# A banded-attention and sine-MLP kernel on one core: batch 0's last x copies moved to ScalarE, its first matmuls started in the attention tail, GpSimd squares in the first MLP pass, and one step width in the last pass

## The chip, the cores and the metric

The kernel runs on one core of one Trainium2 chip. Its time is device microseconds (us) of one execution; of a kernel that was run several times, the median is given. An execution that was profiled has a span (first to last instruction of the trace) and, beside it, the same time as the others. TensorE is called PE in profiles, VectorE DVE, ScalarE ACT, GpSimd POOL, SyncE SP. PEld is PE's loading of weights.

## The reference

Attention in chunks of 32 queries with a little context and 8 memory keys, over 4 batches, 8 heads, 768 positions, 64 values a head; then, over the 3072 tokens with 512 features, an MLP whose activation is h + sin(alpha h)^2 / alpha:

```python
for c in range(nc):                       # 24 chunks of 32 queries
    k_ctx = k[:, :, l_start:r_end]        # 16 positions to the left, 8 to the right
    k_full = np.concatenate([mem_k, k_ctx], axis=2)
    v_full = np.concatenate([mem_v, v_ctx], axis=2)
    scores = scale * np.matmul(q_c, k_full.transpose(0, 1, 3, 2))
    a = softmax(scores)                   # written out with max, exp, sum
    out[:, :, c_start:c_end] = np.matmul(a, v_full)
x = out.transpose(0, 2, 1, 3).reshape(3072, 512)
h = x @ w_in                              # 512 x 2048
s = np.sin(alpha * h)
g = h + s * s / (alpha + 1e-09)
return g @ w_out                          # 2048 x 512
```

## The kernel before

**Stages.** The order on every engine is the order in which the program text issues instructions; nothing is rescheduled, and each engine works through its own queue in that order. There are four batches. For batch 0 the program first transposes k and q, then runs `burst(0)`, the attention; for each batch `i` there follows the first MLP layer ("pass i": 16 steps `ft`, each 128 of the 2048 hidden features, over the batch's 768 tokens), and beside it the second layer of the batch before and the preparation of the next. During pass 0 there is no second layer to interleave yet. After pass 0 come eight transposes (`t_k`, `t_q`, "pieces") for batch 1, mixed with second-layer matmuls of batch 0, and then `burst(1)`.

**Attention.** `burst` handles 8 blocks `j` of 96 queries in a software pipeline: scores and exp of block s (`qk_exp`, L262), the product with v of block s-lag (`pv`, L282: PE, then DVE's reciprocal L292 and scaling L293), and in the step after that `xt` (L300): four PE transposes (L306) and one DVE copy (L309) into `xT`, 96 of its 768 token columns. In batch 0, lag is 2, and one idle matmul (`spin`, L167) runs in each step.

**A step of the first layer** is `l1` (L333). PE makes hT with 8 matmuls (4 slices of 128 features, two halves of 384 tokens, L341). ACT makes u = sin(alpha h) (L353). The square s2 = u*u is made by the engine that a letter names: A for ACT (L356), D for DVE (L362), P for POOL (L358). Then DVE makes gT = s2/alpha + h (L370). The letters stand in one string for each pass:

```python
sq = ("ADADADAAADADADAA" if i == 0 else "ADAAPDADADAPADAD")[ft]
```

DVE's part (`finish`) of step ft is issued just before the matmuls of step ft+1. In PSUM, hT has a pool `big` of three buffers that scores, attention outputs and transposes share; in pass 0 the steps 3, 7 and 11 (`split`) use two buffers `hs` of the pool `smp` (two buffers) instead, and their Sin and gT run in two halves (L350, L366). u and s2 have three buffers each. So PE can't begin a step before DVE's gT of the third unsplit step before it is done.

**Second layer.** `l2` (L376) makes 128 tokens with 16 matmuls (L398) and hands each matmul back as one item of a `Stream`; the last item of a block also issues the copy out of PSUM (DVE L405 or ACT L407) and the store from SP's queue. `stream.take(n)` issues n items, and stops early at the end of a block, carrying the rest over. In passes 1 and 2 each step but the first is preceded by `take(2)`, in pass 3 by `take(3)`.

**Loads.** Weights, k, q and v are loaded and cast by DMAs issued from POOL's queue; the program's semaphores for them rotate over eight, so a load issued there waits until the one eight before it has landed. In order after the v blocks of batch 0: eight loads of w_in (256 columns each, L212), k and q of batch 1 (L115), four loads of w_out (4 steps' rows each, L218), four of v (L139 to L148). The memory values `memv_f` are cast once on ACT (L418, all batches, among the first transposes), and `put_memv` (L152, L153, DVE) spreads them into a v buffer for each batch.

**Tables.** ACT holds one table of functions at a time. The load for Sin stands just ahead of the first Sin of each pass, the load for Exp ahead of the first Exp of each burst; copies run under either.

Of the kernel before, what the change touches and what calls it, by code (L numbers as in the profile page):

```python
# [9 lines left out]
P = 128  # L10
QW = 96
# [3 lines left out]
F32 = mybir.dt.float32  # L15
# [30 lines left out]
def kernel(  # L46
# [12 lines left out]
    nc = tc.nc  # L59
    B, H, S, D = q.shape  # L60
# [6 lines left out]
    KT = d_model // P  # L67
    NSUB = S // P
    HALF = S // 2
# [7 lines left out]
    big = ctx.enter_context(tc.tile_pool(name="big", bufs=3, space=bass.MemoryType.PSUM))  # L77
    smp = ctx.enter_context(tc.tile_pool(name="smp", bufs=2, space=bass.MemoryType.PSUM))
# [13 lines left out]
    memv_st = consts.tile([P, B, H, D], BF, name="memv_st")  # L92
    memk_f = gp.tile([32, H, D], F32, name="memk_f", tag="gT")
    memv_f = gp.tile([P, B, H, D], F32, name="memv_f", tag="gT")
    w_in_sb = consts.tile([P, KT, d_ff], BF, name="w_in_sb")
    w_out_sb = consts.tile([P, FT, d_model], BF, name="w_out_sb")
# [70 lines left out]
    def spin(n):  # L167

        z = smp.tile([P, 512], F32, name="z", tag="sm")
        for _ in range(n):  # L170
            nc.tensor.matmul(z[:], zeros[:, 0:P], zeros[:])  # L171
# [36 lines left out]
    for pt in pts:  # L208
        nc.vector.memset(pt[:, H * QW:H * QW + 32], 0.0)

    def load_w_in(c):
        nc.gpsimd.dma_start(  # L212
            w_in_sb[:, :, 256 * c:256 * c + 256],
            moe_w_in[:, 256 * c:256 * c + 256].rearrange("(kt p) f -> p kt f", p=P),
        )

    def load_w_out(c):
        nc.gpsimd.dma_start(  # L218
            w_out_sb[:, 4 * c:4 * c + 4, :],
            moe_w_out[512 * c:512 * c + 512].rearrange("(ft p) o -> p ft o", p=P),  # L220
        )


# [76 lines left out]
    def xt(xT, j, x_blk, ot):  # L300
        if ot is None:
            xtp = smp.tile([P, KT, QW], BF, name="xtp", tag="sm")[:]
        else:
            xtp = ot[:].bitcast(BF)[:, 0, 640:640 + KT * QW].rearrange("p (k c) -> p k c", k=KT)
        for kt in range(KT):
            nc.tensor.transpose(  # L306
                xtp[:, kt, :], x_blk[:, 2 * kt:2 * kt + 2, :].rearrange("p e d -> p (e d)"), ident[0:QW, 0:QW]
            )
        nc.vector.tensor_copy(xT[:, :, QW * j:QW * j + QW], xtp)  # L309

    def burst(b, stream, shares, lag):

        xT = xp.tile([P, KT, S], BF, name="xT")
        ptl, xbl = {}, {}
        for s in range(NJ + lag + 1):
            n = shares[s] if s < len(shares) else 0
            if s < NJ:
                ptl[s] = qk_exp(s)
            if b == 0:
                spin(1)  # L320
            stream.take(n // 3, True)
            if 0 <= s - lag < NJ:
                xbl[s - lag] = pv(b, s - lag, ptl.pop(s - lag))
                if b == 0:
                    xbl[s - lag] = (xbl[s - lag][0], None)
            stream.take((n + 1) // 3, True)
            if 0 <= s - lag - 1 < NJ:
                xt(xT, s - lag - 1, *xbl.pop(s - lag - 1))
            stream.take((n + 2) // 3, True)
        return xT  # L330


    def l1(i, ft, xT, gT, sq, split=False):  # L333
        if split:
            hts = [smp.tile([P, 512], F32, name="hs", tag="sm") for _ in range(2)]
        else:
            hT = big.tile([P, 2, 512], F32, name="hT", tag="big")
            hts = [hT[:, 0], hT[:, 1]]
        for kt in range(KT):
            for hf in range(2):  # L340
                nc.tensor.matmul(  # L341
                    hts[hf][:, 0:HALF],
                    w_in_sb[:, kt, P * ft:P * ft + P],
                    xT[:, kt, HALF * hf:HALF * hf + HALF],
                    start=(kt == 0), stop=(kt == KT - 1),
                )
        u = mlp.tile([P, 2, HALF], F32, name="u")
        if split:
            for hf in range(2):
                nc.scalar.activation(  # L350
                    u[:, hf], hts[hf][:, 0:HALF], ACTF.Sin, scale=alpha_sb[:, ft:ft + 1])
        else:
            nc.scalar.activation(u[:], hT[:, :, 0:HALF], ACTF.Sin, scale=alpha_sb[:, ft:ft + 1])  # L353
        s2 = mlp.tile([P, 2, HALF], F32, name="s2")
        if sq == "A":
            nc.scalar.activation(s2[:], u[:], ACTF.Square)  # L356
        elif sq == "P":
            nc.gpsimd.tensor_tensor(out=s2[:], in0=u[:], in1=u[:], op=ALU.mult)  # L358

        def finish():  # L360
            if sq == "D":
                nc.vector.tensor_tensor(out=s2[:], in0=u[:], in1=u[:], op=ALU.mult)  # L362
            gv = gT[:, ft, :].rearrange("p (e c) -> p e c", e=2)
            for hf in range(2):
                if split:
                    nc.vector.scalar_tensor_tensor(  # L366
                        out=gv[:, hf], in0=s2[:, hf], scalar=inv_alpha[:, ft:ft + 1],
                        in1=hts[hf][:, 0:HALF], op0=ALU.mult, op1=ALU.add)
                elif hf == 0:
                    nc.vector.scalar_tensor_tensor(  # L370
                        out=gv, in0=s2[:], scalar=inv_alpha[:, ft:ft + 1],
                        in1=hT[:, :, 0:HALF], op0=ALU.mult, op1=ALU.add)

        return finish
# [39 lines left out]
    for n in range(2 * HP):  # L414
        (t_k if n % 2 == 0 else t_q)(prs[n], n // 2)
        spin(2)
        if n == 3:
            nc.scalar.copy(memv_st[64:72], memv_f[64:72])  # L418
        if n == 1:
            mt = smp.tile([P, HP, 32], BF, name="mt", tag="sm")  # L420
            for hp in range(HP):
                nc.tensor.transpose(
                    mt[:, hp, :],
                    memk_bf[0:32, 2 * hp:2 * hp + 2, :].rearrange("p e d -> p (e d)"),
                    ident[0:32, 0:32])
        if n + 2 < 2 * HP:
            prs.append(pair_up(kq[n % 2], (n + 2) // 2, first[n + 2]))
        if n == 1:
            nc.vector.tensor_copy(memkT[:], mt[:])
            put_memk(0)  # L430
    put_memv(0)
    nc.vector.reciprocal(inv_alpha[:], alpha_sb[:])
    for c in range(8):
        load_w_in(c)
    kq_next = load_qk(1)
    for c in range(4):
        load_w_out(c)
    load_v_all(1)

    stream = Stream()  # L440
    xT = burst(0, stream, (), 2)
    put_memk(1)
    put_memv(1)

    for i in range(B):
        gT = gp.tile([P, FT, S], BF, name="gT")
        last = i == B - 1
        at_ft = {2 * n: n for n in range(8)}
        pieces = []
        if not last:  # L450
            srcs = [(kq_next[n % 2], n // 2) for n in range(2 * HP)]
        state["pools"] = 1

        def pair_to(n):
            while len(pieces) < min(n, 2 * HP):
                pieces.append(pair_up(*srcs[len(pieces)], nc.vector.tensor_copy if i == 0 and len(pieces) % 2 == 0 else None))

        def piece(n):
            pair_to(n + 3)
            (t_k if n % 2 == 0 else t_q)(pieces[n], n // 2)  # L460

        if 0 < i < B - 1:
            pair_to(2)
        finish = None
        for ft in range(FT):
            sq = ("ADADADAAADADADAA" if i == 0 else "ADAAPDADADAPADAD")[ft]
            if 1 <= ft:
                stream.take(3 if last else 2)
            if 0 < i < B - 1 and ft in at_ft:
                piece(at_ft[ft])  # L470
            if i == 0 and ft == 14:
                pair_to(3)
            if finish is not None:
                finish()
            finish = l1(i, ft, xT, gT, sq, i == 0 and ft in (3, 7, 11))
        finish()
        stream.add(l2(i, gT, last))
        if not last:
            if i == 0:
                state["pools"], state["t"] = 3, 0  # L480
                stream.take(4)
                for n in range(2 * HP):
                    piece(n)
                    stream.take(3, True)
            if i + 2 < B:
                kq_next = load_qk(i + 2)
            if i == 0:
                xT = burst(i + 1, stream, (3, 3, 3, 4, 4, 4, 4, 4, 4, 4, 5, 5), 3)
            else:
                xT = burst(i + 1, stream, (16, 8, 6, 6, 6, 5, 5, 5, 5, 5), 1)  # L490
            if i + 2 < B:
                put_memk(i + 2)
            stream.take(3)
            if i + 2 < B:
                load_v_all(i + 2)
                put_memv(i + 2)
# [31 lines left out]
```

The softmax here doesn't subtract the row's maximum and nothing guards it: scores larger than these inputs give would overflow.

## Time and profile before

| | |
|---|---|
| Time, median of 11 runs | 237.36 us (235.92 to 238.54) |
| The profiled execution's own time | 236.68 us |
| Its span | 234.9 us |
| Granted TensorE clock | full over the whole span |
| PE busy | 217.9 us, 93% of the span |
| DVE, ACT, POOL busy | 160.9, 153.8, 73.1 us |
| Chain that ended last | PE 61%, DVE 14%, ACT 11% of the span |

Read with it: PE's busy time counts pipelined matmuls, so 93% isn't PE at its peak. The trace gives start and length in us for each instruction, and in brackets how long its engine had been idle and which instruction ended that. The profile's chain is followed back from the last instruction, at each step to what released it.

The stages, from the timeline: attention of batch 0 up to 29.5 us, pass 0 from there to about 55, transposes for batch 1 to 61.5, burst(1) to 81, pass 1 to 109.6, burst(2) to 131.4, pass 2 to 161.1, burst(3) to 182.5, pass 3 to 214, and the rest of the second layer to the end.

### The profile page before, as it was taken

Reading aid. Unit: us, or ns where it says so; the run is one execution under the profiler, and the core shown is the slowest. Engines: PE = TensorE matmul, PEld = TensorE weight load, DVE = VectorE, ACT = ScalarE, POOL = GpSimd, SP = SyncE. Lnnn points to the kernel's source line nnn. Section 1 sums busy time; section 2 is a strip of 40 time slices with the busy share of each in tenths; the row PEclk is TensorE's granted clock in tenths of the full one; section 3 lists DMA queues with packets and bytes.
Section 4 is the critical chain, followed back from the end, with each engine's and each line's share of the span. In section 5 each row is a group of like instructions: output and inputs, shape, how many; then the busy total and the mean of one; then the engine's idle time right before and its main releaser. Section 6 shows DMA issues by size and latency. Waiting matters only on the chain.

```text
span 234.9 us, 4493 instructions
## 1 busy us (share of the span) xinstructions
PE 217.9 (93%) x1785; PEld 122.1 (52%) x1785; DVE 160.9 (69%) x287; ACT 153.8 (65%) x237; POOL 73.1 (31%) x96
## 2 busy tenths in 40 slices
PE   6588899989989999998999999998999999899994
PEld 2255555545545556564455656564555555453453
DVE  3586969999338877988557598978466358875110
ACT  2579679984795397899664787779564676880000
POOL 7899975404832115139120115120000020010000
PEclk9999999999999999999999999999999999999999
DMA  5999999999999910019999101001111110101122
GB/s 71 158 144 85 136 189 203 206 207 159 144 217 160 156 45 3 0 46 130 183 149 114 47 0 45 3 0 45 47 45 47 46 45 3 45 0 45 59 78 89
DMA packets 53852, 21.11 MB, mean 90 GB/s; under 512 B 36296, under 2 KB 50888, under 8 KB 53832
## 3 DMA queue, kind: packets, MB, share of 16 engines
q0 software_dynamic: 47616, 14.40, 71.8%
q1 hardware_dynamic: 6216, 6.43, 9.3%
q8 instruction: 14, 0.23, 0.4%
q14 instruction: 6, 0.05, 0.1%
HBM read 28.91 MB, written 6.29 MB: 150 GB/s over the span
## 4 chain that ended last, share of the span: by engine, by line
PE 61%; DVE 14%; ACT 11%; issue 6%; DMA 3%; POOL 2%; POOLq 1%; DVEq 0%; ACTq 0%
PE o L398 30%; PE hT L341 19%; DVE gT L370 6%; ACT pt L275 4%; ACT u L353 3%; DMA q_bf<-in_q_dram 3%; PE ot L288 3%; PE sc L266 3%; DVE s L362 3%; ACT s L356 2%; PE ot L306 2%; PE o L387 1%; DVE x_blk L293 1%; PE tt_a L257 1%; PE tt_a L242 1%
## 5 line engine op out<-in xcount | busy, mean ns | idle before, releaser
L398 PE MATMUL o<-w_out_sb,gT 128*128 128x512 bf16 x368 | 98.3, 380 | 0.6 <-DVE gT L370 0.4
L341 PE MATMUL hT<-xT,w_in_sb 128*128 128x384 bf16 x488 | 87.3, 326 | 3.7 <-DVE gT L370 3.3
L370 DVE SCALAR_TENSOR_TENSOR gT<-s,inv_alpha,hT 128x768 bf16<-128x768 f32 x61 | 60.8, 1012 | 21.6 <-ACT s L356 13.6
L353 ACT ACTIVATE u<-hT,alpha_sb 128x768 f32<-128x768 f32 x61 | 54.7, 898 | 25.4 <-PE hT L341 24.4
L341 PEld LDWEIGHTS <-w_in_sb 128*128 128x128 bf16 x512 | 49.3, 98 | 38.4 <-issue 4.6
L275 ACT ACTIVATE pt<-sc,biasm 128x256 bf16<-128x256 f32 x96 | 37.6, 493 | 12.5 <-PE sc L266 12.4
L398 PEld LDWEIGHTS <-gT 128*128 128x128 bf16 x368 | 31.9, 98 | 26.2 <-DVE gT L370 1.2
L358 POOL TENSOR_TENSOR s<-u 128x768 f32<-128x768 f32 x6 | 8.8, 1466 | 71.6 <-ACT u L353 61.3
L356 ACT ACTIVATE s<-u 128x768 f32<-128x768 f32 x34 | 28.7, 843 | 1.1
L362 DVE TENSOR_TENSOR s<-u 128x768 f32<-128x768 f32 x24 | 24.8, 1033 | 0.7 <-ACT u L353 0.5
L293 DVE TENSOR_TENSOR x_blk<-ot,rinv 96x512 bf16<-96x512 f32 x32 | 22.0, 686 | 1.1
L226 POOL COPY pr<-q_bf 128x768 bf16<-128x768 bf16 x12 | 10.1, 840 | 40.1 <-PE tt_a L242 23.3
L292 DVE RECIPROCAL rinv<-ot 96x8 f32<-96x8 f32 x32 | 6.5, 202 | 20.1 <-PE ot L288 19.7
L407 ACT COPY o_sb<-o 128x512 f32<-128x512 f32 x11 | 6.4, 586 | 20.0 <-PE o L398 20.0
L405 DVE COPY o_sb<-o 128x512 f32<-128x512 f32 x12 | 8.3, 688 | 15.4 <-PE o L398 15.0
L288 PEld LDWEIGHTS <-pt 128*128 128x128 bf16 x256 | 11.9, 97 | 7.3 <-issue 2.3
L266 PEld LDWEIGHTS <-kTi 64*128 64x128 bf16 x256 | 7.0, 94 | 13.3 <-issue 6.8
L171 PE MATMUL z<-zeros 128*128 128x512 bf16 x37 | 12.7, 424 | 1.3 <-DVE zeros L165 1.3
L288 PE MATMUL ot<-vw,pt 128*128 128x65 bf16 x256 | 13.0, 193 | 0.8 <-ACT pt L275 0.6
L266 PE MATMUL sc<-qT,kTi 64*128 64x96 bf16 x256 | 11.4, 205 | 2.1 <-ACT pt L275 1.2
L306 PEld LDWEIGHTS <-x_blk 96*128 96x128 bf16 x128 | 8.4, 97 | 6.6 <-DVE x_blk L293 1.6
L226 POOL COPY pr<-k_bf 128x768 bf16<-128x768 bf16 x8 | 6.6, 825 | 10.7 <-PE tt_a L257 5.8
(66 smaller groups left out, 181.3 us busy)
## 6 DMA issues: line engine op xcount, KB each, us to landing
out_dram<-o_sb SPq DMA_DIRECT2D x23, 256.0 KB, 2.6
k_bf<-in_k_dram POOLq DMA_DIRECT2D x3, 768.0 KB, 8.8
q_bf<-in_q_dram POOLq DMA_DIRECT2D x3, 768.0 KB, 13.3
vw<-in_v_dram POOLq DMA_DIRECT2D x6, 384.0 KB, 17.0
w_in_sb<-in_moe_w_in_dram POOLq DMA_DIRECT2D x8, 256.0 KB, 7.9
w_out_sb<-in_moe_w_out_dram POOLq DMA_DIRECT2D x4, 512.0 KB, 18.5
k_bf<-in_k_dram POOLq DMA_DIRECT2D x4, 192.0 KB, 6.3
q_bf<-in_q_dram POOLq DMA_DIRECT2D x4, 192.0 KB, 6.8
```

The source lines that it names most:

```text
L226: (eng or nc.gpsimd.tensor_copy)(pr[:].rearrange("p r e d -> p e r d"), src[:, 2 * hp:2 * hp + 2])
L266: nc.tensor.matmul(sc[:, e, QW * hp:QW * hp + QW], kTi[64 * e:64 * e + 64, hp, 104 * j:104 * j + P], qT[64 * e:64 * e + 64, hp, QW * j:QW ...
L275: nc.scalar.activation(pt[:, 0:H * QW].rearrange("p (g e c) -> p e g c", g=4, e=2)[:, :, :, 32 * m:32 * m + 32], sc[:, :, 0:4 * QW].rearra ...
L288: nc.tensor.matmul(otv[:, h // 4, h % 4, :], pt[:, QW * h:QW * h + P], vws[b % 2][:, h, j, 0:D + 1])
L293: nc.vector.tensor_tensor(out=x_blk[:].rearrange("p (g e) d -> p g e d", g=2), in0=otv[0:QW, :, :, 0:D], in1=rv.unsqueeze(3).to_broadcast( ...
L306: nc.tensor.transpose(xtp[:, kt, :], x_blk[:, 2 * kt:2 * kt + 2, :].rearrange("p e d -> p (e d)"), ident[0:QW, 0:QW])
L341: nc.tensor.matmul(hts[hf][:, 0:HALF], w_in_sb[:, kt, P * ft:P * ft + P], xT[:, kt, HALF * hf:HALF * hf + HALF], start=(kt == 0), stop=(kt ...
L353: nc.scalar.activation(u[:], hT[:, :, 0:HALF], ACTF.Sin, scale=alpha_sb[:, ft:ft + 1])
L356: nc.scalar.activation(s2[:], u[:], ACTF.Square)
L362: nc.vector.tensor_tensor(out=s2[:], in0=u[:], in1=u[:], op=ALU.mult)
L370: nc.vector.scalar_tensor_tensor(out=gv, in0=s2[:], scalar=inv_alpha[:, ft:ft + 1], in1=hT[:, :, 0:HALF], op0=ALU.mult, op1=ALU.add)
L398: nc.tensor.matmul(o[:], gT[:, ft, P * s:P * s + P], w_out_sb[:, ft, :], start=(ft == 0), stop=(ft == FT - 1),)
```

## The change

- `xt` copies the blocks j = 5, 6, 7 of batch 0 to `xT` on ACT instead of DVE.
- In step 9 of `burst(0)`, a hook issues the four matmuls of steps ft = 0 (between `pv` of block 7 and `xt` of block 6) and ft = 1 (after `xt` of block 6) on the first half of the tokens, which needs blocks 0 to 3 only. Their other half is issued by `l1` as before.
- The eight loads of w_in become five (256, 256, 512, 512, 512 columns), the four of w_out two.
- The cast of `memv_f` on ACT is cut: batch 0's quarter stays where it was, the other three quarters are issued after `burst(0)`, ahead of the first Sin.
- The letters of pass 0 change: 10 squares on ACT and 6 on DVE become 8 on ACT (steps 0, 2, 4, 5, 9, 11, 14, 15), 4 on DVE (1, 3, 7, 13) and 4 on POOL (6, 8, 10, 12).
- In pass 3 `stream.take(3)` becomes `take(2)`, as in the passes before it.

```diff
-    def load_w_in(c):
...
+    def load_w_in(c0, c1):
...
+            w_in_sb[:, :, c0:c1],
...
-            w_out_sb[:, 4 * c:4 * c + 4, :],
+            w_out_sb[:, 8 * c:8 * c + 8, :],
...
-        nc.vector.tensor_copy(xT[:, :, QW * j:QW * j + QW], xtp)
+        (nc.scalar.copy if ot is None and j >= 5 else nc.vector.tensor_copy)(
+            xT[:, :, QW * j:QW * j + QW], xtp)
...
+            if hook:
+                hook(s, 0, xT)
             stream.take((n + 1) // 3, True)
             if 0 <= s - lag - 1 < NJ:
                 xt(xT, s - lag - 1, *xbl.pop(s - lag - 1))
+            if hook:
+                hook(s, 1, xT)
...
+    def l1_mm(hts, ft, xT, kt, hf):
+        nc.tensor.matmul(
+            hts[hf][:, 0:HALF],
+            w_in_sb[:, kt, P * ft:P * ft + P],
+            xT[:, kt, HALF * hf:HALF * hf + HALF],
+            start=(kt == 0), stop=(kt == KT - 1),
+        )
...
-            nc.scalar.copy(memv_st[64:72], memv_f[64:72])
+            nc.scalar.copy(memv_st[64:72, 0], memv_f[64:72, 0])
...
-    for c in range(8):
-        load_w_in(c)
+    for c0, c1 in ((0, 256), (256, 512), (512, 1024), (1024, 1536), (1536, 2048)):
+        load_w_in(c0, c1)
     kq_next = load_qk(1)
-    for c in range(4):
+    for c in range(2):
         load_w_out(c)
...
+    def early(s, point, xT):
+        ft = {(9, 0): 0, (9, 1): 1}.get((s, point))
+        if ft is not None:
+            opened[ft] = l1_open(ft)
+            for kt in range(KT):
+                l1_mm(opened[ft], ft, xT, kt, 0)
+
+    xT = burst(0, stream, (), 2, early)
+    nc.scalar.copy(memv_st[64:72, 1:B], memv_f[64:72, 1:B])
     put_memk(1)
     put_memv(1)
...
-            sq = ("ADADADAAADADADAA" if i == 0 else "ADAAPDADADAPADAD")[ft]
+            sq = ("ADADAAPDPAPAPDAA" if i == 0 else "ADAAPDADADAPADAD")[ft]
             if 1 <= ft:
-                stream.take(3 if last else 2)
+                stream.take(2)
```

In the changed program ACT's queue at the end of batch 0's attention reads: the last Exp, the three copies to `xT`, the cast of the three quarters of `memv_f`, the table load for Sin, the first Sin. POOL's queue reads: loads up to the last of v, the four squares, then the first `pair_up` copy for batch 1. The order on SP's queue is unchanged.

More of the change, by code (lines that the diff above doesn't have):

```diff
@@ L209 @@
         nc.vector.memset(pt[:, H * QW:H * QW + 32], 0.0)
-    def load_w_in(c):
+    def load_w_in(c0, c1):
         nc.gpsimd.dma_start(
-            w_in_sb[:, :, 256 * c:256 * c + 256],
-            moe_w_in[:, 256 * c:256 * c + 256].rearrange("(kt p) f -> p kt f", p=P),
+            w_in_sb[:, :, c0:c1],
+            moe_w_in[:, c0:c1].rearrange("(kt p) f -> p kt f", p=P),
         )
@@ L218, in load_w_out @@
         nc.gpsimd.dma_start(
-            w_out_sb[:, 4 * c:4 * c + 4, :],
-            moe_w_out[512 * c:512 * c + 512].rearrange("(ft p) o -> p ft o", p=P),
+            w_out_sb[:, 8 * c:8 * c + 8, :],
+            moe_w_out[1024 * c:1024 * c + 1024].rearrange("(ft p) o -> p ft o", p=P),
         )
@@ L308, in xt, with burst @@
             )
-        nc.vector.tensor_copy(xT[:, :, QW * j:QW * j + QW], xtp)
-    def burst(b, stream, shares, lag):
+        (nc.scalar.copy if ot is None and j >= 5 else nc.vector.tensor_copy)(
+            xT[:, :, QW * j:QW * j + QW], xtp)
+    def burst(b, stream, shares, lag, hook=None):
         xT = xp.tile([P, KT, S], BF, name="xT")
@@ L328, in burst, with l1_open, l1 @@
                 xt(xT, s - lag - 1, *xbl.pop(s - lag - 1))
+            if hook:
+                hook(s, 1, xT)
             stream.take((n + 2) // 3, True)
         return xT
-    def l1(i, ft, xT, gT, sq, split=False):
+    def l1_open(ft, split=False):
         if split:
[L335 to L338, printed above, removed]
-        for kt in range(KT):
[L340 to L346, printed above, removed]
+            return [smp.tile([P, 512], F32, name="hs", tag="sm") for _ in range(2)]
+        hT = big.tile([P, 2, 512], F32, name="hT", tag="big")
+        return [hT[:, 0], hT[:, 1], hT]
+    def l1_mm(hts, ft, xT, kt, hf):
[5 more added lines that the diff above has]
+        )
+    def l1(ft, xT, gT, sq, hts, halves, split=False):
+        for kt in range(KT):
+            for hf in halves:
+                l1_mm(hts, ft, xT, kt, hf)
+        hT = None if split else hts[2]
         u = mlp.tile([P, 2, HALF], F32, name="u")
@@ L440 @@
     stream = Stream()
-    xT = burst(0, stream, (), 2)
+    opened = {}
+    def early(s, point, xT):
[6 more added lines that the diff above has]
+    nc.scalar.copy(memv_st[64:72, 1:B], memv_f[64:72, 1:B])
     put_memk(1)
@@ L474 @@
                 finish()
-            finish = l1(i, ft, xT, gT, sq, i == 0 and ft in (3, 7, 11))
+            split = i == 0 and ft in (3, 7, 11)
+            if ft in opened:
+                finish = l1(ft, xT, gT, sq, opened.pop(ft), (1,))
+            else:
+                finish = l1(ft, xT, gT, sq, l1_open(ft, split), (0, 1), split)
         finish()
```

## The prediction

> **What bounds the kernel now.** I read the page first, then the timeline of each stage that the change touches, then the chain of waits. The page says that PE carries the chain, but by stages it doesn't always:
>
> ```profile
> PE 61%; DVE 14%; ACT 11%; issue 6%; DMA 3%; POOL 2%; POOLq 1%; DVEq 0%; ACTq 0%
> L356 ACT ACTIVATE s<-u 128x768 f32<-128x768 f32 x34 | 28.7, 843 | 1.1
> L362 DVE TENSOR_TENSOR s<-u 128x768 f32<-128x768 f32 x24 | 24.8, 1033 | 0.7 <-ACT u L353 0.5
> L358 POOL TENSOR_TENSOR s<-u 128x768 f32<-128x768 f32 x6 | 8.8, 1466 | 71.6 <-ACT u L353 61.3
> ```
>
> PE's 61% lies in passes 1 to 3 and the second layer; DVE and ACT carry most of the chain in pass 0. The three squares cost 0.84 us on ACT, 0.95 on DVE undisturbed (the shortest of the 24 is 0.948), 1.47 on POOL.
>
> The timeline of the hand-over into pass 0:
>
> ```profile
> 26.21 1.28 ACT L353 ACT_TABLE_LOAD   x1
> 28.73 0.34 PE L306 MATMUL xtp<-ident,x_blk 96*128 96x96 bf16 x4 [0.46 <-DVE x_blk L293]
> 29.11 0.36 DVE L309 COPY xT<-xtp 128x384 bf16<-128x384 bf16 x1 [0.17 <-PE xtp L306]
> 29.52 3.90 PE L341 MATMUL hT<-xT,w_in_sb 128*128 128x384 bf16 x23 [0.28 <-DVE xT L309]
> 30.86 0.90 ACT L353 ACTIVATE u<-hT,alpha_sb 128x768 f32<-128x768 f32 x1 [3.37 <-PE hT L341]
> ```
>
> ACT loads the Sin table at 26.21, right after the last Exp, and then idles 3.37 us: today the load is hidden completely. From 30.86 on ACT runs without a pause until 51.6, while PE waits for DVE's gT before step 15 (1.14 us). So pass 0 is bound by ACT and DVE together.
>
> **Rule for walking a pass.** From these rows: a step's 8 matmuls take PE 1.30, and Sin can start 0.2 after; Sin holds ACT 0.92 (split 0.93), a square 0.76; gT holds DVE 0.93 (split 1.05) and is done after 1.01 (1.14); DVE's square takes 0.95 and 0.07 to gT. Buffers free as the code has them (three unsplit hT, three u, three s2). Walking the old letters from 29.52 gives step 15's hT at 50.79 (trace 50.90), its Sin at 52.29 (52.40). That is good enough for differences.
>
> **1. Tail of the attention and first Sin.** DVE loses three copies (0.36 each, 0.27 of it exclusive), so x_blk of block 7 is done near 28.4 instead of 28.68. But PE now does step 0's half (4 x 0.1625 = 0.65, from 27.25 to 27.90; its w_in landed at 22.05 + 4.4 = 26.45), xt of block 6 (0.27), step 1's half (0.65) and the spin, so xt of block 7 starts at about 29.04 instead of 28.73 and ends at 29.38. ACT's copy I take at 0.48 (the 768-column copy L258 takes 0.80; 384 columns fewer at 0.83 ns): xT is complete at 29.90 instead of 29.47. Behind that copy now stand two things. The cast:
>
> ```profile
> 13.15 1.90 ACT L418 CAST memv_st<-memv_f 8x2048 bf16<-8x2048 f32 x1
> ```
>
> 512 columns cost 0.62 (L200), 2048 cost 1.90, so 1536 cost 1.47: to 31.37. Then the table load, which stands ahead of Sin in the queue and so loses its cover: 1.28, to 32.65. First Sin at 32.70 instead of 30.86: **+1.84**. The queue behind it is all of pass 0's Sins and squares; put_memv on DVE also waits for the cast, until 32.6, but gT is not due before 34.5. The quarter of the cast left at 13.15 saves 1.28 there for nobody: the first Exp waits for the last qT, whose transposes end at 16.06. For the load the trace has a row with work right behind it: at 62.02, and the next Exp starts at 63.31, 1.29 later. [...]
>
> The early matmuls buy nothing: PE is through step 3 at 33.85 and then waits until step 0's gT frees its buffer (34.51 + 1.06 = 35.57), 1.72 us.
>
> **2. The letters.** ACT has two squares fewer (1.5), DVE two fewer (2.0). In place stand four of 1.47 on POOL, each about 0.12 after its Sin. DVE works in order, so every gT behind a POOL square waits for it, and so does PE through its buffer. The walk with the new letters (start in us; sq on the engine of the letter):
>
> | step | hT | u | sq | gT |
> |---|---|---|---|---|
> | 0 A | 29.95 | 32.70 | 33.62 | 34.51 |
> | 4 A | 35.57 | 37.91 | 38.83 | 40.39 |
> | 6 P | 38.82 | 41.27 | 42.29 | 43.80 |
> | 7 D | 40.53 | 42.19 | 44.73 | 46.69 |
> | 8 P | 41.83 | 43.33 | 44.35 | 47.74 |
> | 10 P | 44.86 | 46.66 | 47.86 | 49.60 |
> | 11 A | 47.88 | 49.38 | 50.31 | 51.20 |
> | 12 P | 49.18 | 51.07 | 52.09 | 53.60 |
> | 13 D | 50.48 | 51.99 | 55.06 | 56.08 |
> | 15 A | 54.66 | 56.16 | 57.08 | 57.97 |
>
> Step 11 waits for step 7's gT (hs), step 15 for step 12's. Old letters put gT of step 15 at 54.10. The difference is 3.87: 1.84 from the start; **+1.09** from waits for POOL squares (the same walk with 0.95 for step 7's square gives 2.93); and **+0.94** because step 7's DVE square meets step 8's POOL square. For that there is a row:
>
> ```profile
> 92.34 1.01 DVE L370 SCALAR_TENSOR_TENSOR gT<-s,inv_alpha,hT 128x768 bf16<-128x768 f32 x1 [1.55 <-POOL s L358]
> 93.02 0.82 POOL L226 COPY pr<-k_bf 128x768 bf16<-128x768 bf16 x1
> 93.27 1.38 DVE L362 TENSOR_TENSOR s<-u 128x768 f32<-128x768 f32 x1
> ```
>
> The square that starts inside a POOL copy takes 1.38 and ends about 0.81 after it; the gT that began beside another POOL copy (92.25) takes its usual 1.01. No row has a square on both engines at once, so 0 to 0.94; I take 0.94, by the same instruction. [...]
>
> **3. Loads.** POOL issues five DMAs fewer (0.75 each) and no longer waits for k and q to land (idle 2.49 and 3.12 before L145 and L148). Its loads end near 38.2, when the last w_in has landed (37.2), so before the first POOL square at 42.3: off the path. Landings stay, since the DMA engines move about 205 GB/s without a gap from 34 to 54, and w_in's pieces are due well after (step 4 at 35.6, landed by 32). The larger w_out pieces are a new wait only if pass 0 is not late: rows for step 8 are wanted at 54.7 in the old order and would land with the last at 34.85 + 20.4 = 55.25 instead of 52.7. In the forecast they are wanted after 58, so nothing.
>
> **4. After pass 0.** The transposes for batch 1 start when step 13's gT frees a buffer (53.42 in the trace), and from there PE, DVE and the table load at 62.02 follow one another without slack, so the 3.87 goes through to the end.
>
> **5. Pass 3, take(3) to take(2).** 26 second-layer matmuls are left. Before, they are spent by step 9, and then steps 9 to 15 go bare at the pace of ACT, DVE and one POOL square:
>
> ```profile
> 204.59 2.76 PE L341 MATMUL hT<-xT,w_in_sb 128*128 128x384 bf16 x16 [0.88 <-DVE gT L370]
> 205.05 1.47 POOL L358 TENSOR_TENSOR s<-u 128x768 f32<-128x768 f32 x1 [11.25 <-ACT u L353]
> 214.05 2.33 PE L398 MATMUL o<-w_out_sb,gT 128*128 128x512 bf16 x10 [0.38 <-DVE gT L370]
> ```
>
> With 2, a step takes 1.30 + 2 x 0.215 = 1.73 up to step 13 (182.46 + 13 x 1.73 = 204.95), ACT keeps pace, steps 14 and 15 start at 206.4 and 207.7, and the last gT ends at 212.66 (Sin 209.39, square 210.60, gT 211.65). The walk of the old widths gives 213.88 for the resumption (trace 214.05), of the new 212.72: **-1.16**. Bounds: 0, and -1.90 (pass 2, which uses 2, takes 29.69 from first matmul to resumption, pass 3 takes 31.59).
>
> **Sum.** 3.87 - 1.16 = +2.71. The profiled execution took 236.68 (span 234.9 and 1.78 around it): 239.39. The median of the runs is 0.68 higher, so 240.07, say 240.1. About 0.5% (1.19 us) is what a measurement can tell from no change.
>
> **Rivals.**
> - *POOL squares are slower than their rows*, being beside loads and DVE: at 1.9 the walk gives 4.73, so 237.36 + 4.73 - 1.16 = 240.9. All six rows lie within 1.46 to 1.47, against it.
> - *The late start alone counts*, or is partly recovered because ACT has less to do: +1.84 - 1.16, so 238.0; with waits and no blocking (2.93) 239.1. For it: POOL waits show only in a walk.
> - *Faster*: ACT's sum decides pass 0. ACT's work falls from 22.35 to 20.83; without any pause it ends at 53.53 instead of 53.97, so -0.44 and 237.36 - 0.44 - 1.16 = 235.8. The point where it decides: the three hT buffers must cover each POOL square, which they do only if DVE isn't kept waiting for more than about 0.3 a time. Against it, DVE waited 0.33 to 1.55 behind all six POOL squares of today.
> - *The change does not do what it says*: early matmuls and fewer loads hide nothing that is on the path. I have priced both at zero already.
>
> **Chances.** Forecast with or without the blocking (239.0 to 240.7) 0.55; slower POOL 0.12; late start alone and the like 0.22; faster 0.11. The range 236.9 to 241.6 leaves out the faster case and the end of the slow one. Faster by over 0.5%: 0.10; within 0.5%: 0.15; slower: 0.75.
>
> **What would show it.** Right: a table load at about 31.4 and the first Sin near 32.7; PE idle about 1.7 before step 4; a DVE square of 1.9 at step 7; the first transposes for batch 1 at 57.3; pass 3 resuming 30.3 after its first matmul. Wrong: the load still near 26, no DVE waits behind POOL squares of pass 0, or transposes before 55.

## The result, and the profile after

The changed kernel takes 239.0 us (median of 13 runs, 238.16 to 240.3); the kernel before, in the 48 runs beside it, 237.31. The ratio is 1.0071, 95% interval 1.0049 to 1.0092: slower by 0.7%. The profiled execution took 238.36 with a span of 236.5, against 236.68 and 234.9.

The page's chain and the groups of squares (busy us, mean ns of one, then idle us of the engine ahead of them):

```profile
PE 62%; ACT 13%; DVE 10%; issue 7%; POOL 3%; DMA 3%; POOLq 1%; DVEq 0%; ACTq 0%
L368 POOL TENSOR_TENSOR s<-u 128x768 f32<-128x768 f32 x10 | 14.7, 1466 | 78.1 <-ACT u L363 65.7
L366 ACT ACTIVATE s<-u 128x768 f32<-128x768 f32 x32 | 27.0, 844 | 1.0
L372 DVE TENSOR_TENSOR s<-u 128x768 f32<-128x768 f32 x22 | 23.9, 1086 | 0.5 <-ACT u L363 0.5
```

POOL's squares are no slower than before (1466 ns, ten of them now), and ACT's are the same. DVE's mean has risen from 1033 to 1086 though it has two fewer. By share the chain moved from DVE to ACT and POOL.

The hand-over into pass 0, from the timeline (start, length, in brackets the idle time ahead of it and what ended it):

```profile
28.27 0.34 PE L306 MATMUL xtp<-ident,x_blk 96*128 96x96 bf16 x4
...
28.64 0.48 ACT L309 COPY xT<-xtp 128x384 bf16<-128x384 bf16 x1 [0.56 <-PE xtp L306]
29.15 1.47 ACT L462 CAST memv_st<-memv_f 8x1536 bf16<-8x1536 f32 x1
...
30.63 1.28 ACT L363 ACT_TABLE_LOAD   x1
...
31.93 0.90 ACT L363 ACTIVATE u<-hT,alpha_sb 128x768 f32<-128x768 f32 x1
...
34.80 0.48 PE L345 MATMUL hT<-xT,w_in_sb 128*128 128x384 bf16 x2 [1.35 <-DVE gT L380]
```

Copy, cast, table load and Sin follow one another on ACT without a gap; the 3.37 us that ACT idled here before are gone. PE is ready long before and then waits 1.35 for a buffer.

The chain of waits of the same execution, from there on (pieces in order of time):

```profile
29.15 1.47 ACT memv_st L462
...
41.32 1.47 POOL s L368
...
43.74 1.98 DVE s L372
...
51.02 1.47 POOL s L368
52.52 1.03 DVE gT L380
53.55 0.04 issue
53.59 1.48 PE hT L345 x8
```

The cast, two POOL squares and one DVE square of double length now stand in the chain up to the end of pass 0. Pass 3 at its end:

```profile
207.64 4.35 PE L345 MATMUL hT<-xT,w_in_sb 128*128 128x384 bf16 x24
211.82 3.40 PE L408 MATMUL o<-w_out_sb,gT 128*128 128x512 bf16 x15
215.65 4.71 PE L408 MATMUL o<-w_out_sb,gT 128*128 128x512 bf16 x21 [0.43 <-DVE gT L380]
```

The last three steps run through without a wait; before, PE waited 0.88 at 204.59, inside the pass.

**Stages.** Read from the timelines of all profiled executions: E is the first Exp, S the first Sin, T the first transposes for batch 1, P the first matmul of pass 3, R the resumption of the second layer after the last gT. From R to the end every run takes 20.83 to 20.92.

| run | E | E to S | S to T | T to P | P to R | E to T | median us (runs) |
|---|---|---|---|---|---|---|---|
| before | 17.27 | 13.59 | 22.56 | 128.88 | 31.75 | 36.15 | 237.31 (48) |
| after | 16.49 | 15.44 | 24.18 | 128.86 | 30.68 | 39.62 | 239.0 (13) |
| e1 | 16.56 | 15.32 | 22.42 | 128.96 | 30.68 | 37.74 | 237.19 (10) |
| e2 | 17.53 | 13.82 | 23.17 | 128.85 | 30.68 | 36.99 | 236.37 (10) |
| e3 | 17.36 | 13.41 | 24.18 | 128.85 | 30.68 | 37.59 | 236.91 (10) |
| e4 | 17.27 | 15.32 | 24.18 | 128.85 | 31.75 | 39.50 | 240.05 (4) |
| e5 | 19.28 | 13.59 | 22.57 | 128.88 | 30.67 | 36.16 | 236.44 (12) |
| e6 | 18.16 | 13.41 | 21.20 | 130.52 | 30.68 | 34.61 | 235.92 (12) |
| e7 | 17.37 | 15.33 | 23.10 | 128.86 | 30.68 | 38.43 | 238.0 (1) |
| e8 | 18.99 | 15.32 | 26.81 | 128.85 | 30.68 | 42.13 | 243.33 (1) |
| e9 | 16.48 | 13.41 | 21.20 | 129.47 | 30.68 | 34.61 | 234.56 (6) |
| e10 | 18.20 | 14.86 | 24.18 | 128.85 | 30.68 | 39.04 | 239.43 (1) |
| e11 | 17.91 | 13.51 | 21.70 | 128.84 | 30.69 | 35.21 | 235.22 (1) |
| e12 | 16.66 | 13.59 | 22.56 | 128.89 | 31.75 | 36.15 | 237.28 (12) |

The stages repeat within about 0.1 us from run to run: E to S of the changed kernel is 15.44 here, and 15.32 or 15.33 in the four runs with the same queue on ACT (e1, e4, e7, e8). The first Exp doesn't repeat: it lies anywhere from 16.48 to 19.28, though the programs differ ahead of it only in the length of one cast. So a cause is read from the stages, and the medians stand beside it.

### The profile page after: what moved, and what is told of

Same layout as the page of the kernel before. It is cut to its first block, busy times and chain, and to the rows that moved or that the text cites. A ratio compares the mean times of both kernels' runs of the same rounds, so it can differ in the third digit from the quotient of the medians.

```text
span 236.5 us, 4494 instructions
## 1 busy us (share of the span) xinstructions
PE 218.5 (92%) x1785; PEld 122.1 (52%) x1785; DVE 158.6 (67%) x282; ACT 154.1 (65%) x239; POOL 75.2 (32%) x95
## 4 chain that ended last, share of the span: by engine, by line
PE 62%; ACT 13%; DVE 10%; issue 7%; POOL 3%; DMA 3%; POOLq 1%; DVEq 0%; ACTq 0%
PE o L408 30%; PE hT L345 20%; DVE gT L380 5%; ACT pt L275 4%; ACT u L363 4%; PE ot L288 3%; DMA q_bf<-in_q_dram 3%; PE sc L266 3%; DVE s L372 2%; POOL s L368 2%; ACT s L366 2%; PE ot L306 2%; PE o L397 1%; PE tt_a L257 1%; PE tt_a L242 1%
## 5 line engine op out<-in xcount | busy, mean ns | idle before, releaser
L368 POOL TENSOR_TENSOR s<-u 128x768 f32<-128x768 f32 x10 | 14.7, 1466 | 78.1 <-ACT u L363 65.7
L366 ACT ACTIVATE s<-u 128x768 f32<-128x768 f32 x32 | 27.0, 844 | 1.0
L372 DVE TENSOR_TENSOR s<-u 128x768 f32<-128x768 f32 x22 | 23.9, 1086 | 0.5 <-ACT u L363 0.5
L257 PEld LDWEIGHTS <-pr 128*128 128x128 bf16 x96 | 6.5, 98 | 6.1 <-ACT pr L226 3.1
```

## Experiments

The kernels e1 to e4, e7, e8 and e10 are the changed kernel with the edit shown or named; e5 and e12 are the kernel before with it. e6 builds on e3, e9 on e6, and e11 on e9. The kernels e7, e8, e10 and e11 ran once.

**e1: the old letters.**

```diff
-            sq = ("ADADAAPDPAPAPDAA" if i == 0 else "ADAAPDADADAPADAD")[ft]
+            sq = ("ADADADAAADADADAA" if i == 0 else "ADAAPDADADAPADAD")[ft]
```

> The changed kernel with the letters of pass 0 as they were (no POOL squares in pass 0). Stage A is the time from the first Exp to the first transposes for batch 1: 36.15 us in the kernel before, 39.62 in the changed one. My theory: the letters cost 2.03 of the forecast's 3.87 (1.09 waits, 0.94 a blocked DVE square), so stage A falls to about 37.7 (37.4 to 38.1) and the time to some 2.0 us under the changed kernel's, about 237.0. Rival, only the late first Sin counts: stage A stays near 39.5 and the time near 239.

Measured: ratio 1.0002 (0.9966 to 1.0037). S to T falls by 1.76 to 22.42 and the late first Sin stays. So the letters cost 1.76. With the old letters S to T is 0.14 shorter here than in the kernel before (22.56); that the late Sin is the cause was not tested by itself.

**e2: the whole cast at the start again.**

```diff
-            nc.scalar.copy(memv_st[64:72, 0], memv_f[64:72, 0])
+            nc.scalar.copy(memv_st[64:72], memv_f[64:72])
...
-    nc.scalar.copy(memv_st[64:72, 1:B], memv_f[64:72, 1:B])
```

> The changed kernel with the whole cast of memv_f back among the first transposes. My theory: the first Sin comes 1.47 us earlier, and stage A falls by as much, to about 38.15; the first Exp doesn't move for it. Rival, POOL squares are the bound and swallow the start: stage A stays above 39.3. Second question: in the two traces so far the first Exp is at 17.27 (before) and 16.49 (changed). If the shorter cast moves it, it is near 17.3 here; if it is scatter of the first loads, it follows the landing of q and is anywhere from 16.4 to 17.4.

Measured: ratio 0.9964 (0.9941 to 0.9987). E to S falls by 1.62, the cast (1.47) and a little more. S to T falls too, by 1.01, though the letters are the changed ones. The timelines show the difference, first the changed kernel's, then e2's:

```profile
43.43 1.47 POOL L368 TENSOR_TENSOR s<-u 128x768 f32<-128x768 f32 x1 [0.65 <-ACT u L363]
43.74 1.97 DVE L372 TENSOR_TENSOR s<-u 128x768 f32<-128x768 f32 x1
```

```profile
43.16 2.28 POOL L368 TENSOR_TENSOR s<-u 128x768 f32<-128x768 f32 x1 [0.96 <-ACT u L363]
43.16 0.95 DVE L372 TENSOR_TENSOR s<-u 128x768 f32<-128x768 f32 x1
```

In e2 steps 7 and 8 have their squares at the same instant, DVE gets through in its usual 0.95, and POOL's takes 2.28 instead of 1.47. In the changed kernel POOL's came 0.31 earlier than DVE's, and DVE's took 1.97.

**e3: e2, and the Sin table loaded ahead of the last x copies.**

```diff
+            if b == 0 and s == NJ - 1:
+                warm = consts.tile([P, 1], F32, name="warm")
+                nc.scalar.activation(warm[:], zeros[:, 0:1], ACTF.Sin)
```

> The changed kernel with the whole cast back among the first transposes, and with a Sin of one column issued right after the last Exp, which brings the Sin table load ahead of the copies to xT. My theory: first Sin 2 us or more earlier than in the changed kernel, now bound by its matmuls; stage A falls by 1.84 or a little more, to 37.5 to 37.8, the rest being the letters. Rival, the start is not on the path: stage A stays above 39.3. Rival, the load costs where it stands now because the copies wait behind it: first Sin gains under 1 us over the run with the cast alone moved.

Measured: ratio 0.9985 (0.996 to 1.001). E to S is 13.41, now 0.18 under before: with cast and load out of the way, all of the late Sin is gone. But T comes 0.60 later after E than in e2, since POOL's square is first again and DVE's takes 1.98.

**e4: steps of 3 in pass 3 again.**

```diff
-                stream.take(2)
+                stream.take(3 if last else 2)
```

> The changed kernel with take(3) in pass 3. My theory: pass 3 from its first matmul to the resumption of the second layer goes from 30.52 back to 31.6 us, the time rises by 1.1 to about 240.1, stage A stays at 39.6. Rival, the change of pass 3 in the trace is scatter: pass 3 stays under 31.

Measured: 240.05, ratio 1.0149 (1.0104 to 1.0195). P to R is 31.75, as before, and PE waits inside the pass again, with the 0.88 of before:

```profile
207.91 2.76 PE L345 MATMUL hT<-xT,w_in_sb 128*128 128x384 bf16 x16 [0.88 <-DVE gT L380]
210.94 2.81 PE L345 MATMUL hT<-xT,w_in_sb 128*128 128x384 bf16 x16 [0.27 <-DVE gT L380]
```

**e5: the kernel before with steps of 2 alone.** The edit is the reverse of e4's.

> The kernel before with take(2) in pass 3 and nothing else. My theory: pass 3 goes from 31.75 us (first matmul, the early one included, to resumption) to 30.68, all else as in the kernel before, so the median falls by 1.07, ratio 0.9955. Rival: all variants so far were measured 0.5 to 0.7 us faster than the sum of their stages from the first Exp on says; if that lies in how the kernel before scatters and not in what the variants share, this one too comes out 1.6 to 1.8 faster, ratio near 0.993.

Measured: ratio 0.9946 (0.9913 to 0.9978); P to R 30.67, all other stages as before. e4 and e5 put pass 3's part at 1.07 to 1.08, with and without the rest.

**e6: e3 with letters chosen for POOL.**

```diff
-            sq = ("ADADAAPDPAPAPDAA" if i == 0 else "ADAAPDADADAPADAD")[ft]
+            sq = ("DADAADPAPAPAADAA" if i == 0 else "ADAAPDADADAPADAD")[ft]
```

> The changed kernel with the whole cast at the start, the early Sin, and the letters DADAADPAPAPAADAA: POOL squares at 6, 8 and 10 only, and no DVE square near them. By the walk of pass 0 with the durations of the traces, no gT behind a POOL square waits long enough to hold PE, so stage A is 34.8 (34.3 to 35.6), 1.4 under the kernel before, and with pass 3's 1.07 the time is 2.4 under it, about 234.9. Rival, POOL squares cost by themselves: stage A stays at 36.8 or more, as with the letters of the change.

Measured: ratio 0.9936 (0.9898 to 0.9974). E to T is 34.61, 1.54 under before, but T to P is 1.64 longer than in the kernel before. The wait, from PE's timeline:

```profile
56.35 0.59 PE L411 MATMUL o<-w_out_sb,gT 128*128 128x512 bf16 x2 [1.88 <-DMA w_out_sb<-in_moe_w_out_dram]
```

Eight second-layer matmuls are done, the ninth needs step 8's rows, and these are in the second of the two large pieces. In this execution, what pass 0 won is handed back to a load.

**e7: step 7's DVE square with its second input in PSUM.**

```diff
-            if sq == "D":
+            if sq == "D" and split and ft == 7:
+                for hf in range(2):
+                    nc.vector.tensor_tensor(out=s2[:, hf], in0=u[:, hf], in1=hts[hf][:, 0:HALF], op=ALU.mult)
+            elif sq == "D":
```

> The changed kernel, but the DVE square of step 7 multiplies u by hs from PSUM, in two halves, so that it reads only one operand from SBUF (step 7's values are not the reference's). If two SBUF inputs are what makes DVE wait for a POOL square, the two halves take 1.1 to 1.2 together instead of 1.97, and stage A falls from 39.6 by 0.8 to 1.0. Rival, any DVE instruction on SBUF data is held while POOL computes: they take 1.9 or more, and stage A stays.

Measured (timeline):

```profile
44.20 1.47 POOL L368 TENSOR_TENSOR s<-u 128x768 f32<-128x768 f32 x1 [0.66 <-ACT u L363]
44.51 1.01 DVE L373 TENSOR_TENSOR s<-u,hs 128x384 f32<-128x384 f32 x2
```

The same 0.31 behind POOL's square, DVE now takes 1.01 for both halves instead of 1.97, and S to T falls by 1.08. With one of its two inputs in PSUM the square comes through beside POOL's, so POOL's work as such did not hold it. The edit halves the instruction too, and no run halves it with both inputs in SBUF, so the two are not told apart here. gT, which reads one tile from SBUF (hT lies in PSUM), isn't slowed either: in e2 its two halves at 44.15 take their usual 1.14 beside POOL's square. Nor are whole ones, which speaks for the input: in the changed kernel three of them take 2.86 together (2.87 before, without a POOL square), though POOL's square of step 10 starts within the first:

```profile
46.80 2.86 DVE L380 SCALAR_TENSOR_TENSOR gT<-s,inv_alpha,hT 128x768 bf16<-128x768 f32 x3
47.03 1.47 POOL L368 TENSOR_TENSOR s<-u 128x768 f32<-128x768 f32 x1 [2.13 <-DVE gT L376]
```

**e8: the old number of loads.** Eight loads of w_in and four of w_out, as before; all else as changed.

> The changed kernel with eight loads of w_in and four of w_out, as in the kernel before. My theory: the loads are off the path in themselves, but POOL's queue then waits for k and q to land before its last two loads, until about 45 to 46, and the square of step 6 stands behind them, 4 us later than the 41.3 of the changed kernel: stage A rises by 2.5 to 4. Rival, the fewer loads are only fewer instructions: stage A stays at 39.6 within 0.5.

Measured: 243.33; E to T 42.13, 2.51 longer. (The rest of the difference in time is the first Exp, 2.50 later here than in the changed kernel's profile.) POOL's timeline:

```profile
41.51 0.78 POOL L145 DMA_DIRECT2D vw<-in_v_dram  x1 [2.50 <-DMA k_bf<-in_k_dram]
45.41 0.83 POOL L148 DMA_DIRECT2D vw<-in_v_dram  x1 [3.12 <-DMA q_bf<-in_q_dram]
46.27 2.90 POOL L368 TENSOR_TENSOR s<-u 128x768 f32<-128x768 f32 x2
```

POOL's squares stand in the queue behind loads that wait for k and q to land. In the changed kernel POOL's last load is issued at 38.19 and the first square starts at 41.32. So fewer loads gain nothing by themselves (e12), but without them the POOL squares would cost 2.51 more.

**e9: four loads of w_out, and e6's letters.** As e6, with w_out in four pieces, and the last two loads of v for batch 1 moved behind the POOL squares (at step 11), so that no square stands behind a load that waits.

> The letters DADAADPAPAPAADAA with the cast at the start, the Sin table loaded early and steps of 2 in pass 3, as in the run that ended with a wait of 1.88 us for the second w_out half. Now w_out comes in four loads, and the last two loads of v for batch 1 are issued behind the POOL squares (at step 11), so that no load of v stands before a square and waits for k or q. Theory (the wait was the size of the load alone): first Exp to first transposes 34.6 us as there, from there to pass 3 back to 128.9 to 129.4, pass 3 30.7, so 2.1 to 2.6 under before by stages: 234.8 to 235.2 us, ratio about 0.990. Rival (the DMA engines are busy until about 56 whatever the pieces, so that a pass 0 that ends early waits for rows of w_out anyway): the stretch up to pass 3 stays at 130 or more, the gain at 1.3 to 1.5 us, ratio 0.994.

Measured: 234.56, ratio 0.9888 (0.984 to 0.9937): faster than both kernels. E to T repeats at 34.61, and T to P is 129.47, a hair over what was expected. A wait is left, and the chain of waits now runs through a load:

```profile
32.06 22.69 DMA w_out_sb<-in_moe_w_out_dram
54.76 0.04 issue
54.80 0.38 PE o L408
```

PE had waited 0.81. Twelve matmuls came before it, so it is the rows of step 12, the last piece, that are late now. The rival was right about that much: the last rows landed at 54.75 here, no earlier than the second large piece in e12 below (54.7), and only the earlier ones were pulled forward.

**e10: no early matmuls.** The hook is left out (`burst(0, stream, (), 2)`), all else as changed.

> The changed kernel without the early matmuls in the attention tail; all else as changed. Theory (they buy nothing, since PE waits before step 4 in any case and ACT's cast sets the first Sin): first Exp to first Sin 15.1 to 15.4 us against 15.44 (block 7's transposes come earlier by the matmuls that no longer stand before them), first Exp to first transposes 39.2 to 39.6 against 39.62. Rival (they pay part of the late Sin back through PE): 40.3 to 40.9, longer by what the two half steps take.

Measured: E to S 14.86, 0.58 shorter, S to T 24.18 as with them. They do not just buy nothing, they cost 0.58 (0.46 against the four runs with 15.32 or 15.33): the transposes of block 7 start 11.19 after the first Exp instead of 11.78, and the queue of copy, cast and table load starts that much earlier. That is more than I had put down (0.04 to 0.34). The time, 239.43, is longer than the changed kernel's all the same, as the first Exp of this one run came at 18.20.

**e11: e9 without early matmuls.**

> The kernel with four loads of w_out, without the early matmuls. There the first Sin waits for hT, not for ACT. Theory (early matmuls are worth what they take off the way from the last x copy to the first hT, less what they put before block 7's transposes): first Exp to first Sin 13.5 to 13.7 us against 13.4 with them, first Exp to first transposes 34.7 to 35.0 against 34.6. Rival (with Sin no longer late they are worth the half step, 0.65 each): 35.2 or more.

Measured: E to T 35.21, 0.60 longer than e9, so the rival's side of the line. First Sin loses only 0.10; the rest comes at step 1, whose Sin waits for PE:

```profile
30.09 3.90 PE L345 MATMUL hT<-xT,w_in_sb 128*128 128x384 bf16 x23 [0.40 <-ACT xT L306]
...
31.42 0.90 ACT L363 ACTIVATE u<-hT,alpha_sb 128x768 f32<-128x768 f32 x1 [1.39 <-PE hT L345]
32.72 0.90 ACT L363 ACTIVATE u<-hT,alpha_sb 128x768 f32<-128x768 f32 x1 [0.40 <-PE hT L345]
```

The early matmuls gain 0.60 or lose 0.46 to 0.58, by who sets the first Sins: PE (e11) or ACT's queue (e10).

**e12: the new loads alone, in the kernel before.**

> The kernel before with one part of the change alone: five loads of w_in and two of w_out. Its pass 0 isn't late, so the rows of step 8 in the second w_out piece should now be wanted before they land. Theory: first Exp to first transposes 36.1 us as before, and PE waits for w_out behind the first transposes, so that the stretch from there to pass 3 takes 129.4 to 130.8 against 128.9 (0.5 by the prediction's landing at 55.25; 1.9 was the wait in the run with the new letters for POOL); pass 3 31.75; 237.8 to 239.2, ratio 1.002 to 1.008. It also asks where 0.7 us come from that the changed kernels' medians lie under the sum of their stages. Rival A, the loads bring it before the first Exp: then the median comes out 0.7 under the stage sum here as well, ratio 0.999 to 1.005. Rival B, the rows land in time: 128.9, ratio 1.000.

Measured: ratio 1.0015 (0.9991 to 1.0039), and every stage as before. Rival B was right.

```profile
54.73 0.59 PE L398 MATMUL o<-w_out_sb,gT 128*128 128x512 bf16 x2 [0.22 <-DMA w_out_sb<-in_moe_w_out_dram]
```

Step 8's rows were there at 54.73, a wait of 0.22 that cost nothing by the start of pass 3 (128.89). In e6 the same piece, issued at the same time (the two issues start at 27.65 here, at 27.70 there), was there at 56.35. Why that differs by 1.6 between these two executions is not shown. In e6 the rows were wanted at 54.47 (54.09 and one matmul of 0.38), so with e12's landing the wait would have been about 0.3, an estimate.

## Why the prediction was right, and where its sizes were off

It said slower by 2.71, with 240.1 and a range to 241.6; the median rose by 1.7 to 239.0. From the first Exp on the stages say +3.47 in E to T and -1.07 in P to R, together +2.40.

- **Late first Sin.** Forecast 1.84, measured 1.85. The load at 30.63 and the Sin at 31.93 were forecast at about 31.4 and 32.70; this execution's first Exp came 0.78 earlier, so counted from there both are met within 0.02. That closeness is partly luck: the four runs with the same queue are late by 1.73 to 1.74. e2 and e3 show that the cast (1.62 of E to S) and the place of the load (0.41 more) are the cause.
- **Letters, waits and blocking.** Forecast 1.09 + 0.94 = 2.03. Measured 1.76 (e1), less the 0.14 by which e1's S to T is under the kernel before's, so 1.62 in S to T. The blocking is 1.08 (e7), a little above the forecast; the waits are then 0.68, by subtraction, instead of 1.09. That is the term of the sum that was mis-sized. The walk was exact up to step 4, which starts 2.87 after Sin in both; it was 0.2 too long by the first POOL square (9.59 forecast, 9.39 measured), and 0.3 by step 15 (21.96 and 21.66).
- **The blocked square.** The prediction had a DVE square beside a POOL copy to go by. Pairs of squares are in these runs, in both orders: DVE's takes 1.97 behind POOL's (changed kernel), POOL's takes 2.28 beside a DVE square that came through in 0.95 (e2), and in two halves with one input in PSUM DVE's takes 1.01 (e7). The price can be read as a time after the other's end: DVE's square ends 0.81 after POOL's (changed kernel, e3), and POOL's 1.33 after DVE's, in e2 as in e6, where POOL's starts 0.24 before DVE's ends and takes 1.57 (1.56 in e9).
- **Early matmuls.** "Buy nothing" was too kind: 0.46 to 0.58 lost (e10), which is part of the late first Sin. The prediction had 0.31 of that, as a later start of block 7's transposes, but it set this against the kernel before; with the three copies on ACT and no early matmuls they would have started 0.27 earlier than before.
- **Loads.** "Off the path" was right for what was built: POOL's last load starts at 38.19 (forecast: the loads end near 38.2), ahead of the first square. But they are a condition, not a free extra: e8. That the pieces of w_in land well before they are due was not quite so: PE's weights at 30.67 waited 0.43 for one, in the changed kernel's profile alone and without cost, as PE then waits 1.35 for a buffer. The wait for the large w_out piece, forecast only if pass 0 is not late, came in e6 (1.88) and e1 (0.30) and not in the changed kernel; in e12 pass 0 was not late either, and 0.22 of waiting cost nothing.
- **Pass 3.** Forecast -1.16, measured -1.07; resumption 30.52 after the chain's first hT of pass 3 (185.13), forecast 30.3.
- **The start.** The profile came out 1.03 under the forecast of 239.39: 0.4 of it in pass 0, and 0.78 because its first Exp was at 16.49, less 0.09 in pass 3. The prediction carried the first Exp of one execution over as if it were fixed. The medians, too, rose by less than the stages: against the runs of the kernel before beside them, after, e1, e2, e3 and e4 come out 0.5 to 0.7 below what their stages say, e6 0.4; e5, e9 and e12 do not (+0.2, 0.0 and +0.3). Most of this lies outside the span. In all 69 runs of the changed kernel, e1 to e4 and e6 to e11, the time is 1.67 to 1.88 longer than the span. Of the 76 runs of the kernel before beside e1 to e12, 46 have 2.07 to 2.37 there and the others 1.72 to 1.81; beside e9, where nothing is missing, only 2 of 11 have over 2. By the medians of their spans, e1 to e6, e9 and e12 all lie within 0.25 of their stages, and the changed kernel's median span, 237.2, is 2.2 above the 235.0 of those 76 runs (for the 48 runs beside it no spans are known). So the prediction's 1.78 around the span, taken as the same for both kernels, hides some 0.4 of the slowdown. Why the time outside differs stays open. The short cast is not the cause, as e2 and e3 have the long one, nor are the new loads, as 9 of e12's 12 runs have over 2.

Of the rivals, slower POOL squares did not happen (1466 ns). The late start alone would have been e1's stages (+0.6 with pass 3); the letters are clearly in. The faster rival's condition, that DVE is not kept waiting, fails in the changed letters and holds better in e6's, where DVE's waits for POOL are 0.24, 0.78 and 0.73 instead of 1.26, a doubled square and 1.25; there pass 0 does become faster.

## What to carry to other kernels

Price a moved instruction by the cover of what stands behind it: here 1.47 us of cast cost its whole length, since the table load and the first Sin follow it without a gap. Work given to POOL needs its whole queue looked at, loads that wait included, and its order against DVE's squares, one of which took 1.97 instead of 0.95 here. And a part can change sign with the others (the early matmuls, the load sizes), so the parts of a change that lost are worth trying one by one: e9 uses most of them and gains 1.1%.

## What the runs showed of the hardware

PE's pace at the start is not the same in each execution. From the windows of e5 (stretch, its length, busy times of PE, PEld, DVE, ACT and POOL with counts, granted clock, DMA share, GB/s):

```profile
6.00:8.00 2.00, 0.94 (x8) 0.45 (x8) 1.14 (x3) 0.52 (x1) 1.95 (x4) 1.00 1.87 74
8.00:10.00 2.00, 0.54 (x6) 0.55 (x7) 0.47 (x4) 0.83 (x1) 1.43 (x9) 0.66 1.33 169
10.00:12.00 2.00, 2.00 (x16) 1.13 (x15) 0.65 (x3) 1.53 (x2) 1.87 (x3) 0.50 1.32 201
12.00:14.00 2.00, 2.00 (x11) 1.14 (x10) 1.78 (x5) 0.37 (x1) 2.00 (x4) 0.50 1.41 194
```

PE's granted clock is 0.50 there from 10 to 14 us and 0.66 in the stretch before; the six transposes of a piece that start from 9.46 to 14.24 take 0.82 to 0.85, and 0.50 to 0.51 in before's profile, whose clock is 1.00 in the same stretches. PE had idled 1.14 and 1.84 just ahead of e5's first two pieces, 1.70 and 1.41 in before's, so the idle time in the trace does not tell the two apart, and what brought the clock down is not shown. Nor does the granted clock tell all: in e6 (and e10) the first transposes take 0.82 to 0.85 while the rows give 1.00.

```profile
6.78 0.82 PE L242 MATMUL tt_b<-ident,pr 128*128 128x128 bf16 x6 [1.07 <-DVE pr L226]
...
6.00:8.00 2.00, 1.22 (x8) 0.77 (x8) 0.72 (x2) 0.48 (x1) 1.95 (x4) 1.00 1.74 88
```

The first Exp goes with this: it lies at 16.48 to 17.27 in the five profiles where these transposes take 0.50 to 0.53 (for e12 read from ACT's wait for two of them, 0.60 each as in before's), and at 17.27 to 19.28 in the nine that have some of 0.82. The first small load (the memory keys) landed at 3.65 to 3.72 in six profiles and at 4.55 to 4.76 in the other eight, and the first transposes start at 5.91 to 6.14 in the six and at 6.63 to 7.35 in seven of the eight (for e12's there is no row).
